# Decayed attention into a softplus FFN: later units load k and q in 32x32 blocks, and their new state is computed as whole-float32 products

## The chip, the cores and the metric

The kernel runs on one core of a Trainium2 chip. The metric is the device time of one execution in microseconds (us). The engines are PE (matrix products), DVE (vector), ACT (scalar), POOL (GpSimd) and SP, which here only issues transfers (DMAs). Each has a queue of its own that it works off in order; semaphores order the engines among each other.

## The reference, cut to what matters

```python
# q, k, v: (4, 8, 768, 64) float32; w_in: 512 x 2048, w_out: 2048 x 512, in float64
gamma = 1.0 - 2.0 ** (-5.0 - arange(H))
for t in range(S):
    state = gamma * state + einsum('bhd,bhe->bhde', k[:, :, t], v[:, :, t])
    y[:, :, t] = scale * einsum('bhd,bhde->bhe', q[:, :, t], state)
x = y.transpose(0, 2, 1, 3).reshape(3072, 512)
h = x @ w_in
out = (maximum(h, 0) + log1p(exp(-abs(h)))) @ w_out
```

Per head, the attention carries a 64x64 state that decays by gamma with each position. Its output, 3072 tokens of 512, goes through a two-layer FFN with softplus between the layers.

## The kernel before

**Units.** The attention is cut into chunks of 128 positions. A unit is one chunk of one batch for one half of the heads (`hf`, four heads, which are `NJ` = 2 pairs): 4 batches x 6 chunks x 2 halves = 48 units. A unit goes through parts, at the distances in ticks that `PARTS` gives (four ticks from unit to unit):

- `load_unit`: k, q and v of the unit come in as `kn`, `qn`, `vn`, positions on the partitions, one DMA each on SP's queue. `kn` and `qn` have two buffers, `vn` three (`vns`).
- `decay`: POOL multiplies `qn` and `vn` by tables of powers of gamma (`qtabs`, `vtabs`).
- `operands`: PE transposes `kn` and `qn` by pairs of heads into one PSUM tile `tp` (four transposes, L152 and L154), so that the head dimension lies on the partitions.
- `scores`: products of k and q, masked by POOL into `ah` (and `al`).
- `new_state`: the product of k and v is added to a running state in PSUM, `stp`. The last chunk of a batch skips it.
- `stack_and_outputs`: the output `yp`, then copies of the state for the next chunk.

**Early and later units.** Units below `WHOLE` = 12 use whole float32 operands. From unit 12 on, each operand is split into a high part rounded to float32r (a cast on ACT) and the rest (a subtraction on DVE): `kq` for k and q, `vhl` for v, `kh` and `kl` for k as it is needed in `new_state`. A product is then a sum of three: high x high, high x low, low x high.

**FFN.** The 3072 tokens are handled in nine blocks (`BLOCKS`), 2048 hidden features in 16 groups. `hidden` is the first layer (L310 to L312: three products of 128x384 or 128x256 each), `softplus_1` and `softplus_2` run on DVE, ACT and POOL, `second` is the other layer (L341 to L343, 128x512). Until about 110 us the weights also come in and are split (`load_weights`, `convert_weights`).

**What sets the order.** The loops interleave attention ticks and FFN steps by `plan`, and a list scheduler with its own timeline then sets the final order on each engine. On PE the units' products stand between those of the FFN. All loads and stores share SP's queue. Every DMA of SP and ACT uses one of eight semaphores (named DMAHW0 to DMAHW7 in the order below) and waits until the one that used it last has landed.

Of the kernel before, what the change touches and what calls it, by code (L numbers as in the profile page):

```python
# [10 lines left out]
F32 = mybir.dt.float32  # L11
F32R = mybir.dt.float32r
# [3 lines left out]
ALU = mybir.AluOpType  # L16

P = 128
C = 128
# [6 lines left out]
WHOLE = 12  # L26
# [7 lines left out]
def decay_attention_then_softplus_ffn(ctx: ExitStack, tc: tile.TileContext, q, k, v, w_in, w_out, qtab, vtab, gtab, out):  # L34
    nc = tc.nc
    B, H, S, D = q.shape
    DM, DF = w_in.shape
    NC = S // C
# [5 lines left out]
    HH = H // 2  # L44
    NJ = HH // 2

    const = ctx.enter_context(tc.tile_pool(name="const", bufs=1))
    attn = ctx.enter_context(tc.tile_pool(name="attn", bufs=1))
# [8 lines left out]
    gtab_sb = const.tile([P, 2, H], F32, name="gtab_sb")  # L57
    qtabs = const.tile([P, NC, H], F32, name="qtabs")
    vtabs = const.tile([P, NC, H], F32, name="vtabs")
    ident = const.tile([P, P], F32, name="ident")  # L60


# [38 lines left out]
    units = [(c // NC, c % NC, hf) for c in range(B * NC) for hf in range(2)]  # L101
    loads, live, state = {}, {}, {}
# [4 lines left out]
    for i, size in enumerate(BLOCKS):  # L107
        at = (0, 256, 384, 0)[i] if i < 4 else 384 * (i % 2 == 0)
# [4 lines left out]
    lo, up = slice(0, D), slice(D, P)  # L113
# [12 lines left out]
    stp = ps_s.tile([P, 2, NJ, P], F32, name="stp")  # L126
    sides = ((0, lo, up), (1, up, lo))

    def load_unit(n):
        if n in loads:  # L130
            return
        b, c, hf = units[n]
        tiles = []
        for nm, src in (("kn", k), ("qn", q), ("vn", v)):
            t = vns[n % 3][:, :, 0, :] if nm == "vn" else attn.tile([P, HH, D], F32, name=nm, bufs=2)
            nc.sync.dma_start(t, src[b, hf * HH:(hf + 1) * HH, c * C:(c + 1) * C, :].rearrange("h s d -> s h d"))
            tiles.append(t)
        loads[n] = tiles

    def decay(n):  # L140
        b, c, hf = units[n]
        kn, qn, vn = loads[n]
        hs = slice(hf * HH, (hf + 1) * HH)
        nc.gpsimd.tensor_tensor(qn, qn, qtabs[:, c, hs].unsqueeze(2).broadcast_to([P, HH, D]), op=ALU.mult)  # L144
        nc.gpsimd.tensor_tensor(vn, vn, vtabs[:, c, hs].unsqueeze(2).broadcast_to([P, HH, D]), op=ALU.mult)  # L145

    def operands(n):
        b, c, hf = units[n]
        kn, qn, vn = loads.pop(n)
        tp = ps_a.tile([P, 2, NJ, C], F32, name="tp", tag="a")  # L150
        for j in range(NJ):
            nc.tensor.transpose(tp[:, 0, j, :], kn[:, 2 * j:2 * j + 2, :], ident)  # L152
        for j in range(NJ):
            nc.tensor.transpose(tp[:, 1, j, :], qn[:, 2 * j:2 * j + 2, :], ident)  # L154
        if n < WHOLE:
            qt = qs[:, n % 2]
            nc.scalar.copy(kz[lo, 0], tp[lo, 0])
            nc.vector.tensor_copy(kz[up, 1], tp[up, 0])
            nc.scalar.copy(qt, tp[:, 1])
            live[n] = [qt, kn, vn]  # L160
            return
        kq = kqs[n % 2]
        for par, own, oth in sides:
            nc.scalar.copy(kq[own, :2, par], tp[own])  # L164
            nc.scalar.copy(kq[oth, 1, par], tp[own, 1])  # L165
        for par, own, oth in sides:
            nc.vector.tensor_tensor(kq[oth, 0, par], tp[own, 0], kq[own, 0, par].bitcast(F32), op=ALU.subtract)  # L167
            nc.vector.tensor_tensor(kq[own, 2, par], tp[own, 1], kq[own, 1, par].bitcast(F32), op=ALU.subtract)

        vhl = attn.tile([P, HH, 2, D], F32R, name="vhl", tag="vhl", bufs=2)  # L170
        nc.scalar.copy(vhl[:, :, 0, :], vn)
        nc.vector.tensor_tensor(vhl[:, :, 1, :], vn, vhl[:, :, 0, :].bitcast(F32), op=ALU.subtract)
        kh = kl = None
        if c < NC - 1:
            kh = attn.tile([P, HH, D], F32R, name="kh", tag="kh")
            kl = attn.tile([P, HH, D], F32R, name="kl")
            nc.scalar.copy(kh, kn)
            nc.vector.tensor_tensor(kl, kn, kh.bitcast(F32), op=ALU.subtract)
        live[n] = [kq, vhl, kh, kl]

    def scores(n):
        kq = live[n][0]
# [23 lines left out]
    began = {}  # L206

    def new_state(n):
        b, c, hf = units[n]
        live[n].append(state[hf] if c else None)  # L210
        if c == NC - 1:
            return
        for j in range(NJ):
            hs = slice(2 * j, 2 * j + 2)
            if n < WHOLE:
                kn, vn = live[n][1:3]
                products = [(kn, vn)]
            else:
                vhl, kh, kl = live[n][1:4]
                vh, vl = (vhl[:, :, t, :] for t in range(2))  # L220
                products = [(kh, vh), (kh, vl), (kl, vh)]
            for i, (kk, vv) in enumerate(products):

                first = c == 0 and hf == 0 and j == 0 and i == 0
                m = nc.tensor.matmul(  # L225
                    stp[:, hf, j, :], lhsT=kk[:, hs, :], rhs=vv[:, hs, :], start=first, stop=True, skip_group_check=True
                )
                if first:
                    began[b] = m.ins
                elif c == 0:  # L230
                    tc.add_manual_dep(m.ins, began[b].name, mybir.DependencyInfo(mybir.DependencyClass.NoSync, mybir.DependencyReason.DATA), reason="the bank's first")

    def stack_state(n):
        b, c, hf = units[n]
# [14 lines left out]
    def outputs(n):  # L249
        b, c, hf = units[n]  # L250
        kq, *rest, st = live.pop(n)
        off, g = places[n // 2], hf * NJ
        xh, xl = (x[:, g:g + NJ, off:off + C] for x in xring)
        if n < WHOLE:
            kn, vn, a = rest
            yp = ps_a.tile([P, NJ, C], F32, name="yp", tag="a")
            v0 = vns[n % 3].rearrange("p h t d -> p (h t) d")
            for j in range(NJ):
                if c:
                    nc.tensor.matmul(yp[:, j], lhsT=st[:, j, :], rhs=kq[:, j, :], start=True, stop=False)  # L260
                for par in range(2):
                    at = 2 * (2 * j + par) - par
                    nc.tensor.matmul(yp[:, j], lhsT=v0[:, at:at + 2, :], rhs=a[:, 2 * j + par, :], start=c == 0 and par == 0, stop=par == 1)
            nc.scalar.copy(xh, yp)  # L264
            nc.vector.tensor_tensor(xl, yp, xh.bitcast(F32), op=ALU.subtract)
            return
        yp = ps_a.tile([D, 2, NJ, C], F32, name="yp", tag="a")
        vhl, kh, kl, ah, al = rest
        for j in range(NJ):
            for par in range(2):  # L270
                h = 2 * j + par
                o = yp[:, par, j, :]
                if c:
                    nc.tensor.matmul(o, lhsT=st[:, par, j, :], rhs=kq[:, 1, par, j, :], start=True, stop=False)  # L274
                    nc.tensor.matmul(o, lhsT=st[:, par, j, :], rhs=kq[:, 2, par, j, :], start=False, stop=False)  # L275
                nc.tensor.matmul(o, lhsT=vhl[:, h, 0, :], rhs=ah[:, h, :], start=c == 0, stop=False)  # L276
                nc.tensor.matmul(o, lhsT=vhl[:, h, 0, :], rhs=al[:, h, :], start=False, stop=False)  # L277
                nc.tensor.matmul(o, lhsT=vhl[:, h, 1, :], rhs=ah[:, h, :], start=False, stop=True)  # L278
        for par, own, oth in sides:
            nc.scalar.copy(xh[own], yp[:, par])  # L280
        for par, own, oth in sides:
            nc.vector.tensor_tensor(xl[own], yp[:, par], xh[own].bitcast(F32), op=ALU.subtract)
# [8 lines left out]
    PERIOD = 4  # L291
# [72 lines left out]
    for i, a, b in turns:  # L364
        m = WIDE // BLOCKS[i]
        steps += [(i, tuple(range(f, f + m))) for f in range(a, b, m)]

    def ticks_for(i):

        return min(PERIOD * 2 * int(FIRST[i + 1] // C) + max(PARTS) - PERIOD + 1 + AHEAD, last_tick + 1)  # L370

    done, loaded, converted = FIRST_TICK, 0, 0
# [11 lines left out]
    for n in range(2):  # L384
        load_unit(n)
# [16 lines left out]
    for c in range(1, NC):  # L402
        nc.vector.tensor_tensor(qtabs[:, c], qtabs[:, c - 1], gtab_sb[:, 0], op=ALU.mult)
        nc.vector.tensor_tensor(vtabs[:, c], vtabs[:, c - 1], gtab_sb[:, 1], op=ALU.mult)
    while done < ticks_for(0):
        tick(done)
        done += 1
        if done % 4 == 3 and done > 0 or done < 0 and loaded == 0:
            if loaded >= FETCH:
                convert_weights(converted)  # L410
                converted += 1
            load_weights(loaded)
            loaded += 1
# [3 lines left out]
    for a, b in zip(starts, starts[1:]):  # L417
        i = steps[b][0]
# [61 lines left out]
```

## Time and profile before

| | us |
|---|---|
| median of 3 runs | 690.71 (690.22 to 691.65) |
| the profiled execution | 691.96 |
| its span, first to last instruction | 690.2 |
| granted TensorE clock, mean | 0.997 |

The profile is of one execution. Busy time counts each engine by itself; the engines overlap. A row of a group gives the line, engine, operation, output and inputs with shapes, the count, then busy time and the mean of one in ns, then idle time just before these instructions and what ended it. Rows of a timeline begin with start and duration in us. SPq and ACTq are the sequencers that issue DMAs.

### The profile page before, as it was taken

Reading aid. Unit: us, or ns where it says so; the run is one execution under the profiler, and the core shown is the slowest. Engines: PE = TensorE matmul, PEld = TensorE weight load, DVE = VectorE, ACT = ScalarE, POOL = GpSimd, SP = SyncE. Lnnn points to the kernel's source line nnn. Section 1 sums busy time; section 2 is a strip of 40 time slices with the busy share of each in tenths; the row PEclk is TensorE's granted clock in tenths of the full one; section 3 lists DMA queues with packets and bytes.
Section 4 is the critical chain, followed back from the end, with each engine's and each line's share of the span. In section 5 each row is a group of like instructions: output and inputs, shape, how many; then the busy total and the mean of one; then the engine's idle time right before and its main releaser. Section 6 shows DMA issues by size and latency. Waiting matters only on the chain.

```text
span 690.2 us, 12071 instructions
## 1 busy us (share of the span) xinstructions
PE 675.2 (98%) x4340; PEld 618.9 (90%) x4340; DVE 417.0 (60%) x873; ACT 354.5 (51%) x802; POOL 283.0 (41%) x344
## 2 busy tenths in 40 slices
PE   6899999999999999999999999999999999999997
PEld 5798999999999999999999999999999999999996
DVE  5687785756656665566666666666766555533321
ACT  5788775555545544545545546455554544433221
POOL 5687675334443334343433433343333423222221
PEclk9999999999999999999999999999999999999999
DMA  8977632121111121112111121111211101000100
GB/s 244 287 221 223 175 127 47 39 69 55 32 23 39 25 77 24 39 24 62 41 37 24 31 69 39 25 31 27 82 32 24 24 15 62 1 0 1 47 1 30
DMA packets 90746, 42.72 MB, mean 62 GB/s; under 512 B 77376, under 2 KB 85568, under 8 KB 90688
## 3 DMA queue, kind: packets, MB, share of 16 engines
q1 hardware_dynamic: 90240, 41.96, 22.2%
q8 instruction: 34, 0.56, 0.3%
q14 instruction: 24, 0.20, 0.1%
q10 hardware_dynamic: 448, 0.01, 0.0%
HBM read 35.66 MB, written 6.29 MB: 61 GB/s over the span
## 4 chain that ended last, share of the span: by engine, by line
PE 94%; DMA 3%; ACT 1%; SPq 1%; POOL 1%; issue 0%; POOLq 0%
PE hp L310 13%; PE acc L341 13%; PE hp L312 13%; PE hp L311 13%; PE acc L343 13%; PE acc L342 13%; PE stp L225 3%; PE sc L195 3%; PE tp L154 1%; PE tp L152 1%; PE yp L278 1%; PE yp L277 1%; PE yp L276 1%; DMA kn<-in_k_dram 1%; PE yp L275 1%; PE yp L274 1%
## 5 line engine op out<-in xcount | busy, mean ns | idle before, releaser
L326 POOL TENSOR_TENSOR gl<-sp,gh 128x384 fp32r<-128x384 f32 (+1 forms) x120 | 129.2, 1077 | 184.7 <-ACT gh L324 147.6
L310 PE MATMUL hp<-xh,winhl 128*128 128x384 f32 (+1 forms) x576 | 185.9, 323 | 0.5 <-ACT xh L264 0.5
L312 PE MATMUL hp<-xh,winhl 128*128 128x384 f32 (+1 forms) x576 | 184.0, 320 | 0.4 <-POOL winhl L98 0.4
L311 PE MATMUL hp<-xl,winhl 128*128 128x384 f32 (+1 forms) x576 | 183.7, 319 | 0.0
L341 PE MATMUL acc<-wouthl,gh 128*128 128x512 f32 x384 | 154.6, 403 | 0.0
L342 PE MATMUL acc<-wouthl,gh 128*128 128x512 f32 x384 | 151.2, 394 | 0.0
L343 PE MATMUL acc<-wouthl,gl 128*128 128x512 f32 x384 | 150.3, 394 | 0.1
L317 DVE TENSOR_SCALAR sp<-hp 128x384 uint32<-128x384 uint32 (+1 forms) x120 | 69.7, 582 | 111.0 <-PE hp L312 105.7
L318 ACT ACTIVATE sp<-sp 128x384 f32<-128x384 f32 (+1 forms) x120 | 65.4, 546 | 124.1 <-DVE sp L317 123.4
L310 PEld LDWEIGHTS hp<-xh,winhl 128*128 128x128 f32 x576 | 108.8, 189 | 3.9 <-ACT xh L264 0.7
L311 PEld LDWEIGHTS hp<-xl,winhl 128*128 128x128 f32 x576 | 108.9, 189 | 3.2
L312 PEld LDWEIGHTS hp<-xh,winhl 128*128 128x128 f32 x576 | 108.8, 189 | 1.2 <-POOL winhl L98 0.6
L324 ACT CAST gh<-sp 128x384 fp32r<-128x384 f32 (+1 forms) x120 | 64.1, 534 | 86.6 <-DVE sp L322 44.3
L322 DVE SCALAR_TENSOR_TENSOR sp<-hp,sp 128x384 f32<-128x384 f32 (+1 forms) x120 | 69.8, 582 | 34.6 <-ACT sp L318 33.5
L343 PEld LDWEIGHTS acc<-wouthl,gl 128*128 128x128 f32 x384 | 71.8, 188 | 15.0 <-POOL gl L326 0.5
L342 PEld LDWEIGHTS acc<-wouthl,gh 128*128 128x128 f32 x384 | 72.5, 189 | 11.0
L341 PEld LDWEIGHTS acc<-wouthl,gh 128*128 128x128 f32 x384 | 72.3, 188 | 10.5
L144 POOL TENSOR_TENSOR qn<-qn,qtabs 128x256 f32<-128x256 f32 x48 | 29.5, 615 | 97.6 <-DMA qn<-in_q_dram 79.0
L167 DVE TENSOR_TENSOR kq<-tp,kq 64x256 fp32r<-64x256 f32 x72 | 30.4, 422 | 61.3 <-ACT kq L165 60.7
L164 ACT CAST kq<-tp 64x512 fp32r<-64x512 f32 x72 | 41.8, 581 | 38.7 <-PE tp L154 37.7
L145 POOL TENSOR_TENSOR vn<-vn,vtabs 128x256 f32<-128x256 f32 x48 | 29.8, 621 | 67.2 <-DMA vn<-in_v_dram 50.4
L201 POOL TENSOR_SCALAR_AFFINE_SELECT ah<-ah 128x512 fp32r<-128x512 f32 (+1 forms) x48 | 31.4, 654 | 33.3 <-DVE al L198 26.3
(81 smaller groups left out, 1044.6 us busy)
## 6 DMA issues: line engine op xcount, KB each, us to landing
win<-in_moe_w_in_dram SPq DMA_DIRECT2D x16, 512.0 KB, 4.4
wout<-in_moe_w_out_dram SPq DMA_DIRECT2D x16, 512.0 KB, 4.5
kn<-in_k_dram SPq DMA_DIRECT2D x48, 128.0 KB, 2.3
qn<-in_q_dram SPq DMA_DIRECT2D x48, 128.0 KB, 2.7
vn<-in_v_dram SPq DMA_DIRECT2D x48, 128.0 KB, 2.2
out_dram<-o SPq DMA_DIRECT2D x24, 256.0 KB, 2.1
gtab_sb<-in_gtab_dram ACTq DMA_DIRECT2D x2, 2.0 KB, 3.2
qtabs<-in_qtab_dram ACTq DMA_DIRECT2D x1, 4.0 KB, 2.2
```

The lines of the kernel that those rows point to most:

```text
L164: nc.scalar.copy(kq[own, :2, par], tp[own])
L310: nc.tensor.matmul(hp[:, k], lhsT=wt[:, 0, d, :], rhs=xh[:, d, :], start=d == 0, stop=False)
L311: nc.tensor.matmul(hp[:, k], lhsT=wt[:, 0, d, :], rhs=xl[:, d, :], start=False, stop=False)
L312: nc.tensor.matmul(hp[:, k], lhsT=wt[:, 1, d, :], rhs=xh[:, d, :], start=False, stop=d == ND - 1)
L317: nc.vector.tensor_scalar(sp.bitcast(U32), hps[s].bitcast(U32), 0x80000000, None, op0=ALU.bitwise_or)
L318: nc.scalar.activation(sp, sp, AF.Softplus)
L322: nc.vector.scalar_tensor_tensor(g, hps.pop(s), 0.0, g, op0=ALU.max, op1=ALU.add)
L324: nc.scalar.copy(gh, g)
L326: nc.gpsimd.tensor_tensor(gl, sps.pop(s), gh.bitcast(F32), op=ALU.subtract)
L341: nc.tensor.matmul(acc[i][t], lhsT=gh[:, k, ts], rhs=wt[:, 0], start=begins and k == 0, stop=False)
L342: nc.tensor.matmul(acc[i][t], lhsT=gh[:, k, ts], rhs=wt[:, 1], start=False, stop=False)
L343: nc.tensor.matmul(acc[i][t], lhsT=gl[:, k, ts], rhs=wt[:, 0], start=False, stop=ends and f == fs[-1])
```

## The change

**Loads.** For later units q comes in 32x32 blocks instead of as `qn`, and k comes a second time, in blocks, beside `kn`: tiles `kb` and `qb` (`qb` takes the two buffers of `qn`). `load_blocks` issues eight DMAs for each, one per head and half of its 64 columns; a DMA moves 32 x 4 x 32 numbers, in runs of 32 (128 bytes). A later unit has 18 load DMAs on SP instead of three.

**Transposes.** DVE transposes `kb` and `qb` block by block, straight into the PSUM tile `tp`, which gets the same contents as before. PE transposes only the early units.

**Decay.** The positions of q now lie differently, so POOL multiplies `qb` by another table, `qblocks`. Its first chunk is loaded by 16 small DMAs on ACT's queue and extended to the other chunks by ten products on POOL (`block_decays`, called in the first loop after 16 ticks are done).

**New state.** Later units compute it like the early ones, with two float32 products per unit, one per pair of heads, out of `kn` and `vn`; `kh` and `kl` are gone. `kn` and `vn` are now held until then.

```diff
+    def load_blocks(nm, src, b, c, hf):
+        t = attn.tile([P, NJ, C // 32, 32], F32, name=nm, tag={"qb": "qn"}.get(nm, nm), bufs=2)
+        for h in range(HH):
+            for d in range(0, D, 32):
+                at = h % 2 * D + d
+                nc.sync.dma_start(
+                    t[at:at + 32, h // 2], src[b, hf * HH + h, c * C:(c + 1) * C, d:d + 32].rearrange("(i t) d -> t i d", t=32)
+                )
+        return t
...
         for nm, src in (("kn", k), ("qn", q), ("vn", v)):
+            if nm == "qn" and n >= WHOLE:
+                for nm, src in (("kb", k), ("qb", q)):
+                    tiles.append(load_blocks(nm, src, *units[n]))
+                continue
...
+            qb = loads[n][2].rearrange("p m i d -> p (m i) d")
+            by = qblocks[:, c, hf].rearrange("p m i -> p (m i)")
+            nc.gpsimd.tensor_tensor(qb, qb, by.unsqueeze(2).broadcast_to(list(qb.shape)), op=ALU.mult)
...
-        for j in range(NJ):
-            nc.tensor.transpose(tp[:, 0, j, :], kn[:, 2 * j:2 * j + 2, :], ident)
-        for j in range(NJ):
-            nc.tensor.transpose(tp[:, 1, j, :], qn[:, 2 * j:2 * j + 2, :], ident)
         if n < WHOLE:
+            for t, x in enumerate((kn, *rest)):
+                for j in range(NJ):
+                    nc.tensor.transpose(tp[:, t, j, :], x[:, 2 * j:2 * j + 2, :], ident)
...
+        for t, x in enumerate(rest):
+            nc.vector.transpose(tp[:, t].rearrange("p j c -> p (j c)"), x.rearrange("p m i d -> p (m i d)"))
...
-        if c < NC - 1:
-            kh = attn.tile([P, HH, D], F32R, name="kh", tag="kh")
-            kl = attn.tile([P, HH, D], F32R, name="kl")
-            nc.scalar.copy(kh, kn)
-            nc.vector.tensor_tensor(kl, kn, kh.bitcast(F32), op=ALU.subtract)
...
-                products = [(kh, vh), (kh, vl), (kl, vh)]
...
+            m = nc.tensor.matmul(
+                stp[:, hf, j, :], lhsT=kn[:, hs, :], rhs=vn[:, hs, :], start=first, stop=True, skip_group_check=True
+            )
...
+    def block_decays():
+        own = (lo, slice(0, H, 2)), (up, slice(1, H, 2))
+        for at in range(0, P, 32):
+            for i in range(C // 32):
+                nc.scalar.dma_start(
+                    qblocks[at:at + 32, 0, :, :, i].rearrange("p f m -> p (f m)"), qtab[i * 32:(i + 1) * 32, at // D:H:2]
+                )
...
+        if done == PERIOD * 4:
+            block_decays()
```

The scheduler sets the order anew. Three places matter. The first is ACT's queue in the start, with the semaphore waits in brackets. Before, behind the four loads of tables, it stands so (`kz`, `qs`: operands of the first units; `stw`: state; `ah`: scores; `win`, `wout`: weights):

```order
L157 COPY kz<-tp 64x256 [waits PE_49]
L159 COPY qs<-tp 128x256 [waits DVE_49]
L241 COPY stw_87<-stp 64x2x64 [waits DVE_49]
L188 COPY ah<-sc 128x512 [waits PE_49]
L85 ACTIVATE win<-win 128x512 [waits DMAHW2_49]
```

In the changed kernel, at the same place:

```order
L420 DMA qblocks<-in_qtab_dram 32x4x1 [waits DMAHW1_49]
L178 COPY kz<-tp 64x256 [waits PE_49]
L420 DMA qblocks<-in_qtab_dram 32x4x1 [waits DMAHW3_49]
L180 COPY qs<-tp 128x256 [waits DVE_49]
L420 DMA qblocks<-in_qtab_dram 32x4x1 [waits DMAHW5_49]
L251 COPY stw_88<-stp 64x2x64 [waits DVE_49]
L420 DMA qblocks<-in_qtab_dram 32x4x1 [waits DMAHW7_49]
L420 DMA qblocks<-in_qtab_dram 32x4x1 [waits DMAHW1_49]
L205 COPY ah<-sc 128x512 [waits PE_49]
L86 ACTIVATE win<-win 128x512 [waits DMAHW4_49]
```

The 16 loads of `qblocks` are spread over the first 44 instructions of ACT, up to the weights of the third group; each waits for an earlier one, and ACT with it. They take the odd semaphores, so that SP's first loads share the even ones.

The second place is SP's queue in the middle of the program. Before, three loads a unit:

```order
L136 DMA kn<-in_k_dram 128x4x64
L136 DMA qn<-in_q_dram 128x4x64
L136 DMA vn_90<-in_v_dram 128x4x64
L136 DMA kn<-in_k_dram 128x4x64
L136 DMA qn<-in_q_dram 128x4x64
```

In the changed kernel:

```order
L152 DMA kn<-in_k_dram 128x4x64
L136 DMA kb<-in_k_dram 32x4x32 x4
L136 DMA qb<-in_q_dram 32x4x32 x8
L152 DMA vn_92<-in_v_dram 128x4x64
L152 DMA kn<-in_k_dram 128x4x64
L136 DMA kb<-in_k_dram 32x4x32 x8
L136 DMA qb<-in_q_dram 32x4x32 x8
```

Sixteen block loads stand between one `kn` and the next. The first blocks, `kb` of units 12 and 13, have moved far ahead, between the loads of units 5 to 7.

The third place is DVE's queue in the middle. Before (`sp`: softplus of one FFN step; `kq`: the split k and q of a unit; `kl`: the low part of k; `st`: state):

```order
L317 TENSOR_SCALAR sp<-hp 128x384
L167 TENSOR_TENSOR kq_83<-tp,kq_83 64x256
L168 TENSOR_TENSOR kq_83<-tp,kq_83 64x256
L167 TENSOR_TENSOR kq_83<-tp,kq_83 64x256
L168 TENSOR_TENSOR kq_83<-tp,kq_83 64x256
L322 SCALAR_TENSOR_TENSOR sp<-hp,sp 128x384
L178 TENSOR_TENSOR kl<-kn,kh 128x256
```

In the changed kernel:

```order
L327 TENSOR_SCALAR sp<-hp 128x384
L184 STREAM_TRANSPOSE tp<-kb 128x256
L184 STREAM_TRANSPOSE tp<-qb 128x256
L332 SCALAR_TENSOR_TENSOR sp<-hp,sp 128x384
L190 TENSOR_TENSOR kq_85<-tp,kq_85 64x256
L191 TENSOR_TENSOR kq_85<-tp,kq_85 64x256
```

The two transposes stand between the two softplus operations of an FFN step, ahead of the corrections of `kq` that need them, and the subtraction for `kl` is gone.

More of the change, by code (lines that the diff above doesn't have):

```diff
@@ L59, in decay_attention_then_softplus_ffn @@
     vtabs = const.tile([P, NC, H], F32, name="vtabs")
+    qblocks = const.tile([P, NC, 2, NJ, C // 32], F32, name="qblocks")
     ident = const.tile([P, P], F32, name="ident")
@@ L141, in decay @@
         b, c, hf = units[n]
-        kn, qn, vn = loads[n]
+        vn = loads[n][-1]
         hs = slice(hf * HH, (hf + 1) * HH)
-        nc.gpsimd.tensor_tensor(qn, qn, qtabs[:, c, hs].unsqueeze(2).broadcast_to([P, HH, D]), op=ALU.mult)
+        if n < WHOLE:
+            qn = loads[n][1]
+            nc.gpsimd.tensor_tensor(qn, qn, qtabs[:, c, hs].unsqueeze(2).broadcast_to([P, HH, D]), op=ALU.mult)
+        else:
+            qb = loads[n][2].rearrange("p m i d -> p (m i) d")
+            by = qblocks[:, c, hf].rearrange("p m i -> p (m i)")
+            nc.gpsimd.tensor_tensor(qb, qb, by.unsqueeze(2).broadcast_to(list(qb.shape)), op=ALU.mult)
         nc.gpsimd.tensor_tensor(vn, vn, vtabs[:, c, hs].unsqueeze(2).broadcast_to([P, HH, D]), op=ALU.mult)
@@ L148, in operands @@
         b, c, hf = units[n]
-        kn, qn, vn = loads.pop(n)
+        kn, *rest, vn = loads.pop(n)
         tp = ps_a.tile([P, 2, NJ, C], F32, name="tp", tag="a")
-        for j in range(NJ):
-            nc.tensor.transpose(tp[:, 0, j, :], kn[:, 2 * j:2 * j + 2, :], ident)
-        for j in range(NJ):
-            nc.tensor.transpose(tp[:, 1, j, :], qn[:, 2 * j:2 * j + 2, :], ident)
         if n < WHOLE:
+            for t, x in enumerate((kn, *rest)):
+                for j in range(NJ):
+                    nc.tensor.transpose(tp[:, t, j, :], x[:, 2 * j:2 * j + 2, :], ident)
             qt = qs[:, n % 2]
@@ L172, in operands @@
         nc.vector.tensor_tensor(vhl[:, :, 1, :], vn, vhl[:, :, 0, :].bitcast(F32), op=ALU.subtract)
-        kh = kl = None
-        if c < NC - 1:
-            kh = attn.tile([P, HH, D], F32R, name="kh", tag="kh")
-            kl = attn.tile([P, HH, D], F32R, name="kl")
-            nc.scalar.copy(kh, kn)
-            nc.vector.tensor_tensor(kl, kn, kh.bitcast(F32), op=ALU.subtract)
-        live[n] = [kq, vhl, kh, kl]
+        live[n] = [kq, vhl, kn, vn]
     def scores(n):
@@ L212, in new_state @@
             return
+        kn, vn = live[n][1:3] if n < WHOLE else live[n][2:4]
         for j in range(NJ):
             hs = slice(2 * j, 2 * j + 2)
[L215 to L220, printed above, removed]
-                products = [(kh, vh), (kh, vl), (kl, vh)]
[L222 to L231, printed above, removed]
+            first = c == 0 and hf == 0 and j == 0
+            m = nc.tensor.matmul(
+                stp[:, hf, j, :], lhsT=kn[:, hs, :], rhs=vn[:, hs, :], start=first, stop=True, skip_group_check=True
+            )
+            if first:
+                began[b] = m.ins
+            elif c == 0:
+                tc.add_manual_dep(m.ins, began[b].name, mybir.DependencyInfo(mybir.DependencyClass.NoSync, mybir.DependencyReason.DATA), reason="the bank's first")
     def stack_state(n):
@@ L267, in outputs @@
         yp = ps_a.tile([D, 2, NJ, C], F32, name="yp", tag="a")
-        vhl, kh, kl, ah, al = rest
+        vhl, kn, vn, ah, al = rest
         for j in range(NJ):
@@ L404, in decay_attention_then_softplus_ffn @@
         nc.vector.tensor_tensor(vtabs[:, c], vtabs[:, c - 1], gtab_sb[:, 1], op=ALU.mult)
+    def block_decays():
[5 more added lines that the diff above has]
+                )
+        for c in range(1, NC):
+            for half, heads in own:
+                old, new = (qblocks[half, t].rearrange("p f m i -> p (f m) i") for t in (c - 1, c))
+                nc.gpsimd.tensor_tensor(new, old, gtab_sb[half, 0, heads].unsqueeze(2).broadcast_to(list(new.shape)), op=ALU.mult)
     while done < ticks_for(0):
```

## The prediction

> **What bounds the kernel now.** I read the page first (span, busy times, chain that ended last), then busy time by stretches, and only then the order of work on TensorE.
>
> ```profile
> span 690.2 us, 12071 instructions
> ...
> PE 675.2 (98%) x4340; PEld 618.9 (90%) x4340; DVE 417.0 (60%) x873; ACT 354.5 (51%) x802; POOL 283.0 (41%) x344
> ...
> PE 94%; DMA 3%; ACT 1%; SPq 1%; POOL 1%; issue 0%; POOLq 0%
> ```
>
> The matmul engine (PE) is busy for 675.2 of 690.2 us and makes 94% of the chain. A busy PE alone could hide slack, so the second view says where it is ever idle. Its columns are the stretch, its length, then busy time of PE, weight loads, DVE, ACT and POOL, the granted clock, the DMA share and GB/s.
>
> ```profile
> 0.00:10.00 10.00, 5.26 (x21) 4.31 (x22) 3.77 (x19) 2.98 (x6) 4.91 (x17) 1.00 0.78 205
> 10.00:20.00 10.00, 6.40 (x45) 5.44 (x44) 6.87 (x13) 8.26 (x19) 5.96 (x8) 1.00 1.03 296
> 20.00:30.00 10.00, 8.14 (x54) 7.78 (x55) 7.10 (x13) 6.81 (x16) 6.87 (x9) 0.83 1.04 303
> ...
> 200.00:400.00 200.00, 200.00 (x1274) 183.84 (x1273) 125.96 (x277) 101.99 (x245) 76.40 (x98) 1.00 0.15 37
> ...
> 640.00:690.20 50.20, 46.34 (x291) 41.70 (x290) 13.07 (x19) 11.16 (x18) 10.33 (x8) 1.00 0.07 27
> ```
>
> Of the 15.0 us without PE work, 10.2 lie in the first 30 us (4.74 + 3.60 + 1.86) and 3.9 in the last stretch. In between PE runs without a hole (200.00 of 200.00), while DVE has 37% free, ACT 49% and the DMA engines 85%. So there are two regimes: after the start, each nanosecond of PE issue time that goes is a nanosecond of the span; in the start, what counts is ACT and the loads.
>
> **What goes from PE.** In the pipelined order an instruction costs the distance to the next start, not its own duration. The timeline of PE (start, duration) around the four transposes of one later unit:
>
> ```profile
> 302.52 0.35 PE L310 MATMUL hp<-xh,winhl 128*128 128x384 f32 x1
> 302.70 0.34 PE L311 MATMUL hp<-xl,winhl 128*128 128x384 f32 x1
> 302.88 0.34 PE L312 MATMUL hp<-xh,winhl 128*128 128x384 f32 x1
> 303.06 0.38 PE L152 MATMUL tp<-ident,kn 128*128 128x128 f32 x2
> 303.28 0.38 PE L154 MATMUL tp<-ident,qn 128*128 128x128 f32 x2
> 303.42 0.42 PE L310 MATMUL hp<-xh,winhl 128*128 128x384 f32 x1
> 303.67 0.34 PE L311 MATMUL hp<-xl,winhl 128*128 128x384 f32 x1
> ```
>
> Two 128x384 products are 0.18 us apart. From 302.88 to 303.67 stand two of them and the four transposes: 0.79 - 2 x 0.18 = 0.43 us. There are 36 later units (12 to 47), so **36 x 0.43 = 15.5 us** go.
>
> The new state of a later unit, six products of two pairs of heads:
>
> ```profile
> 325.27 0.33 PE L311 MATMUL hp<-xl,winhl 128*128 128x384 f32 x1
> 325.45 0.33 PE L225 MATMUL stp<-vhl,kh 128*128 128x128 f32 x2
> 325.62 0.27 PE L225 MATMUL stp<-vhl,kl 128*128 128x128 f32 x1
> 325.73 0.39 PE L225 MATMUL stp<-vhl,kh 128*128 128x128 f32 x2
> 325.95 0.27 PE L225 MATMUL stp<-vhl,kl 128*128 128x128 f32 x1
> 326.06 0.45 PE L341 MATMUL acc<-wouthl,gh 128*128 128x512 f32 x1
> 326.35 0.40 PE L342 MATMUL acc<-wouthl,gh 128*128 128x512 f32 x1
> 326.58 0.40 PE L195 MATMUL sc<-kq 128*128 128x256 f32 x2
> ```
>
> From 325.27 to 326.35 is 1.08 us; less 0.18 for L311 and 0.23 for a 128x512 product (326.35 to 326.58) it leaves 0.67 us for the six. What takes their place, whole-float32 products, the early units already run:
>
> ```profile
> 42.19 0.61 PE L225 MATMUL stp<-vn,kn 128*128 128x128 f32 x4
> 42.64 0.38 PE L152 MATMUL tp<-ident,kn 128*128 128x128 f32 x2
> ...
> L225 PE MATMUL stp<-vn,kn 128*128 128x128 f32 x40 | 7.2, 307 | 0.0
> ```
>
> 40 instructions for 10 early units: each of a unit's two products is two instructions, and the four take 0.45 us (42.19 to 42.64). The exchange saves 0.67 - 0.45 = 0.22 us. It happens in 30 units, since the last chunk of a batch makes no state (six of the 36): **30 x 0.22 = 6.6 us**. Together 22.1 us.
>
> The Trainium skill speaks against this half: "FP8 and Floating Point Precision", section "TensorE Precision Notes", has true float32 take four passes through the array, against the three products that it replaces here. Four passes at the 0.11 us of one split product would be 2 x 4 x 0.11 = 0.89 us a unit, 0.22 more than now, and the sum of PE would be 15.5 - 6.6 = 8.9 us. The rows differ: four instructions in 0.45 us. That the passes are four they don't contradict; a split product of 128 columns simply costs as much as two of them.
>
> **What is added beside PE.** DVE gets two 32x32-block transposes of 128x256 per unit; the trace has none. ACT loses the copy kh and DVE the subtraction kl in 30 units.
>
> ```profile
> L168 DVE TENSOR_TENSOR kq<-tp,kq 64x256 fp32r<-64x256 f32 x72 | 30.4, 422 | 1.0
> L178 DVE TENSOR_TENSOR kl<-kn,kh 128x256 fp32r<-128x256 f32 x30 | 19.2, 640 | 6.3 <-ACT kh L177 6.3
> ...
> 330.20 0.38 PE L152 MATMUL tp<-ident,kn 128*128 128x128 f32 x2
> ```
>
> Nearest rows for 256 elements a partition: 0.42 (out of PSUM) to 0.64 us; I take 0.43, so DVE gets 36 x 0.86 - 30 x 0.64 = 12 us more in all. A unit lasts (330.20 - 303.06) / 2 = 13.6 us here; at 63% DVE has 5.0 us of it free. The pair stands in DVE's queue between the first and second softplus operation of one FFN step, so these and the corrections of kq wait behind it: about 0.9 us later, hidden by other products that PE has queued. I cost it at nothing; without that cover it is 36 x 0.86 = 31 us. POOL's decay keeps its size, 128x256.
>
> The loads: sixteen transfers of 16 KB take the place of one of 128 KB.
>
> ```profile
> 303.47 0.37 SPq L136 DMA_DIRECT2D kn<-in_k_dram  x1
> 303.94 0.45 SPq L136 DMA_DIRECT2D qn<-in_q_dram  x1
> ...
> L136 SPq DMA_DIRECT2D qn<-in_q_dram x48: 367/448/1312, 1.3 to 569.0; - x48
> ...
> DMA to landing us min/median/max: 2.3/2.7/7.4
> ...
> q1 hardware_dynamic: 90240, 41.96, 22.2%
> ```
>
> SP needs 0.37 to 0.45 us for one, so 18 loads a unit take 6.7 to 8.1 of 13.6 us: SP keeps up. kn now waits for the new-state products of two units before (it waited for kl), and kb and qb queue behind it; but a unit's qn is issued just after the transposes two units earlier (303.94 behind 303.28), some 27 us ahead, and vn, now held until the new state, has three buffers. Sixteen issues, a landing of 2.7 and a decay use about 11 of these. In packets it is 36 x 1536 = 55,296 more, at the present cost of a packet 22.2% x 55,296 / 90,240 = 14% more share of engines that are idle there. Cost nothing; what uncovers it is below.
>
> **What is added in the start.** Sixteen transfers for the block decays stand in ACT's own queue, and 16 blocks of kb for units 12 and 13 among the first loads of SP.
>
> ```profile
> 0.84 0.43 ACTq L387 DMA_DIRECT2D qtabs<-in_qtab_dram  x1
> ...
> 2.43 0.60 ACTq L390 DMA_DIRECT2D gtab_sb<-in_gtab_dram  x1
> ...
> PE sc L187 <- ACT qs L159: 2.3, 5, 0.8
> ```
>
> At the mean of these two, 0.52 us, ACT spends 8.3 us on issuing, interleaved with the copies for which PE waits: the last row has PE waiting five times for qs. Bounds: 0 if all of it falls in ACT's idle time, 8.3 us if none does. Five issues stand ahead of the first ah, where ACT is mostly idle (it is busy for 2.98 us of the first 10); the other eleven, 5.7 us, share a stretch in which ACT is 68 to 83% busy. I take **4.5 us**, with the start's loads inside it: SP's transfers now alternate semaphores with ACT's, so each waits for an earlier one, and the weights of the first FFN steps come some microseconds later. Gains below nothing I exclude: nothing leaves the start.
>
> **Sum.** -15.5 - 6.6 + 4.5 = -17.6 us: a span of 672.6 for the 690.2. The profiled execution took 691.96 us with its ends, 1.25 above the median of 690.71. Against the median: 690.7 - 17.6 = **673.1 us**.
>
> **Rivals.** (1) The start costs nothing: 690.7 - 22.1 = 668.6. For it: the gaps of ACT there; against it: PE's waits for qs.
> (2) DVE's transposes come late for the scores. If each unit's scores waited 0.2 us for kq, 7.2 us come back: 680; if as long as the PE transposes took, 0.43 us, 15.5 come back: 688.6, nearly no change, and the change then does not do what it says. Against it: 5.0 us of DVE free per unit.
> (3) A float32 product costs four split ones (0.89 us a unit): 690.7 - 15.5 + 6.6 + 4.5 = 686.3. Against it: the rows of the early units, 0.45 us.
> (4) The slower side: block loads don't keep pace. The transfers share eight semaphores (DMAHW0 to 7 in the order), so eight are under way at most, and 18 a unit need 18/8 of a landing: 6.1 us at 2.7. PE will need 13.6 - 0.43 - 0.22 = 13.0 us a unit, so the loads bind from a landing of 13.0 x 8/18 = 5.8 us, and have eaten the whole gain, the 4.5 us of the start counted (0.1 a unit), at 13.5 x 8/18 = 6.0. Landings up to 7.4 us stand in the row above, and the start has the DMA share at 1.03; in the middle it is 0.15. At 7 us a unit takes 15.75: 690.7 + 4.5 + 36 x 2.15 = 773 us.
>
> The Trainium skill, "DMA: Bandwidth & Descriptors", section "Anatomy of one DMA — SWDGE (gpsimd) path", puts a fixed cost of about 2.0 us on each transfer whatever its size, which speaks for (4) if they follow each other singly: an estimate of 16 x 2.0 = 32 us a unit. By that rule the trace agrees in size, 2.3 us at least; it does not agree that they queue, since qn was issued 0.47 us behind kn.
>
> **How the numbers follow.** Forecast, PE full and the start dearer by 2 to 8.3 us: 0.62 (670 to 677). (1): 0.14. (2): 0.13, of which 0.03 ends within 0.2% of no change. (3): 0.02. (4): 0.06. Something else in the new order that costs over 5 us but stays faster: 0.03. The range from 667.5, a little below (1) for a differently packed order, to 681.5, with the milder half of (2), leaves out under 0.2. Faster by over 0.2% (what a measurement of this kernel can tell from no change): 0.91; within: 0.03; slower: 0.06. The likeliest time, 673.1, is that of the first case.
>
> **What would show it.** Right: no transposes on PE from unit 12 on, four new-state instructions of 0.11 us where six stood, PE still 200.00 busy of any 200 us in the middle, and idle time in the first 30 us up from 10.2 to about 15. Wrong: PE rows with idle time ended by ACT kq or DVE (2), SP or DVE waiting for DMA kb or qb (4), first FFN products still near 25 us (1). The step that I trust least is the 4.5 us.

## The result and the profile after

| | before | changed |
|---|---|---|
| median us | 690.71 (689.88 to 691.65, 5 runs) | 696.33 (693.88 to 697.0, 5 runs) |
| profiled execution, us | 691.96 | 694.59 |
| its span, us | 690.2 | 692.8 |
| ratio of the times | | 1.007, 95% interval 1.0047 to 1.0093 |

The change made the kernel 0.7% slower. Forecast were 673.1 us and a range of 667.5 to 681.5. First the page of the changed kernel: span, busy times, shares of the chain.

```profile
span 692.8 us, 12604 instructions
...
PE 661.2 (95%) x4136; PEld 600.2 (87%) x4136; DVE 419.2 (61%) x915; ACT 343.1 (50%) x772; POOL 285.1 (41%) x354
...
PE 82%; DMA 6%; DVE 5%; ACT 3%; issue 2%; POOL 1%; SPq 1%; ACTq 0%; DVEq 0%; POOLq 0%
```

PE has 204 records fewer, as it should (4340 - 4136), and 14.0 us less busy time; yet its share of the chain fell from 94% to 82%, and DVE, DMA and ACT came in. The span grew by 2.6 us. The same stretches as before the change:

```profile
0.00:10.00 10.00, 5.34 (x23) 4.28 (x24) 3.54 (x19) 2.94 (x6) 4.92 (x17) 1.00 0.75 187
10.00:20.00 10.00, 3.95 (x29) 3.33 (x29) 6.12 (x12) 6.23 (x14) 4.51 (x9) 0.98 0.89 213
20.00:30.00 10.00, 8.85 (x58) 7.97 (x56) 5.91 (x11) 7.25 (x17) 7.43 (x12) 0.85 0.90 249
200.00:400.00 200.00, 196.90 (x1216) 178.73 (x1215) 128.64 (x296) 98.09 (x236) 77.17 (x99) 1.00 0.24 47
640.00:692.80 52.80, 49.21 (x307) 44.20 (x305) 13.07 (x19) 11.67 (x19) 11.35 (x9) 0.99 0.07 26
```

Two things differ. PE is idle for 11.9 us of the first 30 (10.2 before), and the middle has holes: 196.90 of 200 us, where it had been 200.00. Idle time understates a stall, since the first products behind it are stretched too. So the second measure is the time between two events that every version has: the copies of finished blocks by DVE, `o`. The rows give count, duration, and the first and last start. Before:

```profile
L355 DVE COPY o<-acc x14: 680/692/693, 137.8 to 685.7; 128x512 f32<-128x512 f32 x14
```

In the changed kernel:

```profile
L365 DVE COPY o<-acc x14: 681/688/692, 143.0 to 688.6; 128x512 f32<-128x512 f32 x14
```

The first copy is 5.2 us late. From the first to the last it takes 545.6 us in place of 547.9: 2.3 us were saved there, out of some 21 (worked out below). Where the others went is seen in PE's waits (total, times, longest):

```profile
PE yp L284 <- DVE al L216: 2.9, 4, 0.9
PE yp L284 <- DVE kq L191: 2.6, 1, 2.6
...
PE yp L287 <- POOL al L218: 1.4, 5, 0.3
PE sc L212 <- DVE kq L191: 1.2, 2, 0.9
```

Before, PE had no wait at all from 100 to 640 us. The waits lie near 160, 242, 325, 407, 490 and 574 us: once a block of 384 tokens, where one block's FFN ends and the next begins. I call these places seams. The largest, on DVE (start, duration):

```profile
400.95 0.42 DVE L216 TENSOR_TENSOR al<-sc,al 128x256 fp32r<-128x256 f32 x1
...
401.89 0.45 DVE L184 STREAM_TRANSPOSE tp<-kb 128x256 f32<-128x256 f32 x1
402.37 0.46 DVE L184 STREAM_TRANSPOSE tp<-qb 128x256 f32<-128x256 f32 x1
404.16 0.69 DVE L365 COPY o<-acc 128x512 f32<-128x512 f32 x1 [1.32 <-DMA out_dram<-o]
...
406.64 0.43 DVE L191 TENSOR_TENSOR kq<-tp,kq 64x256 fp32r<-64x256 f32 x1
407.10 0.42 DVE L215 TENSOR_TENSOR al<-sc,ah 128x256 fp32r<-128x256 f32 x1
```

And on PE at the same time:

```profile
402.43 0.48 PE L212 MATMUL sc<-kq 128*128 128x256 f32 x2
...
404.32 0.34 PE L322 MATMUL hp<-xh,winhl 128*128 128x384 f32 x1
407.22 0.24 PE L284 MATMUL yp<-kq,st 128*64 128x128 f32 x1 [2.56 <-DVE kq L191]
407.30 0.22 PE L285 MATMUL yp<-kq,st 128*64 128x128 f32 x1
408.35 0.27 PE L286 MATMUL yp<-ah,vhl 128*64 128x128 f32 x1 [0.83 <-POOL ah L218]
408.60 0.49 PE L320 MATMUL hp<-xh,winhl 128*128 128x384 f32 x1
408.89 0.52 PE L321 MATMUL hp<-xl,winhl 128*128 128x384 f32 x1
409.21 0.52 PE L322 MATMUL hp<-xh,winhl 128*128 128x384 f32 x1
```

A unit's scores come in two pairs of heads, each with its own buffer of a PSUM pool that has two; `tp` and `yp` take theirs from the same pool. At 400.95 the last row of `al` for the unit's first pair starts. Then come the transposes for the next unit, 401.89, and only then this unit's second scores, 402.43. The outputs `yp`, next in PE's queue but for products of the FFN, wait until 407.07 for the last correction of `kq` of the next unit (L191): that is the last reader of `tp`, so `yp` takes over its buffer. Before the change, PE's own queue had the order scores, scores, `tp`, `yp`; the transposes were behind both scores because the same engine ran both.

At four of the other five seams (units 20, 26, 38 and 44) the outputs' first wait is for `al` itself. Near 242 us, on DVE and on PE:

```profile
238.97 0.46 DVE L184 STREAM_TRANSPOSE tp<-kb 128x256 f32<-128x256 f32 x1
239.47 0.46 DVE L184 STREAM_TRANSPOSE tp<-qb 128x256 f32<-128x256 f32 x1
...
241.40 0.41 DVE L216 TENSOR_TENSOR al<-sc,al 128x256 fp32r<-128x256 f32 x1
```

```profile
238.91 0.48 PE L212 MATMUL sc<-kq 128*128 128x256 f32 x2
239.23 0.34 PE L321 MATMUL hp<-xl,winhl 128*128 128x384 f32 x1
...
240.80 0.34 PE L322 MATMUL hp<-xh,winhl 128*128 128x384 f32 x1
241.96 0.24 PE L284 MATMUL yp<-kq,st 128*64 128x128 f32 x1 [0.82 <-DVE al L216]
```

Here the transposes start behind the second scores (238.97 against 238.91), as they do at the seams of units 26, 38 and 44, so `tp` takes no buffer between the scores there. `yp` waits for the second pair's last `al`, which comes late in DVE's queue. Between the scores and the outputs PE's queue holds ten products, some 1.9 us. Counted through the whole order at the distances of the rows, the first unit of each block has little more than that: 3.3 us for unit 14, and 1.9 each for 20, 26, 32, 38 and 44. All other later units have about 5.2 or more; before the change none had less than 5.0. At unit 14, near 160 us, no output waits; the next scores wait 0.3 us for `al`. (The distances named in the expectations below were counted with eight chunks to a batch, where there are six; the counts here are the right ones, and smaller at some units.)

One execution among the experiments, the profiled one of AHEAD = 0, took 1676 us where its other three took 703.56 to 704.61; its trace is not used below.

### The profile page after: what moved, and what is told of

Its sections match the earlier page's. It is cut to its first block, busy times and chain, and to the rows that moved or that the text cites. A ratio compares the mean times of both kernels' runs of the same rounds, so it can differ in the third digit from the quotient of the medians.

```text
span 692.8 us, 12604 instructions
## 1 busy us (share of the span) xinstructions
PE 661.2 (95%) x4136; PEld 600.2 (87%) x4136; DVE 419.2 (61%) x915; ACT 343.1 (50%) x772; POOL 285.1 (41%) x354
## 4 chain that ended last, share of the span: by engine, by line
PE 82%; DMA 6%; DVE 5%; ACT 3%; issue 2%; POOL 1%; SPq 1%; ACTq 0%; DVEq 0%; POOLq 0%
PE hp L320 12%; PE hp L322 12%; PE acc L351 12%; PE acc L352 12%; PE acc L353 12%; PE hp L321 12%; PE sc L212 2%; DMA qblocks<-in_qtab_dram 2%; PE stp L235 2%; DMA wout<-in_moe_w_out_dram 2%; DMA win<-in_moe_w_in_dram 1%; PE yp L287 1%; PE yp L288 1%; PE yp L286 1%; PE yp L273 1%
## 5 line engine op out<-in xcount | busy, mean ns | idle before, releaser
L218 POOL TENSOR_SCALAR_AFFINE_SELECT ah<-ah 128x512 fp32r<-128x512 f32 (+1 forms) x48 | 30.6, 637 | 117.1 <-DVE al L215 104.8
L166 POOL TENSOR_TENSOR qb<-qb,qblocks 128x256 f32<-128x256 f32 x36 | 22.2, 618 | 54.4 <-DMA qb<-in_q_dram 45.5
L292 DVE TENSOR_TENSOR xl<-yp,xh 64x256 fp32r<-64x256 f32 x72 | 30.0, 417 | 17.4 <-ACT xh L290 16.5
```

## The experiments

Times are medians; each ratio is to the kernel before, run on the same chip in turn. The last two columns are the busy time of PE in the first 100 us and from 100 to 640 us of the profiled execution (88.81 and 540.00 before, 82.97 and 529.05 in the changed kernel).

Theories: (1) DVE's queue is too full at the seams; (2) the block loads delay the stores, and so the seams; (3) the new state does it; and, formed on the way, (4) the order in which the transposes now stand; (5) the third output copy, which waits in DVE's queue for a store.

| run | us | ratio (95% interval) | 0 to 100 | 100 to 640 |
|---|---|---|---|---|
| new state alone | 683.77 | 0.9894 (0.9874 to 0.9913) | 89.49 | 540.00 |
| one load each | 687.95 | 0.9949 (0.9929 to 0.9968) | 87.37 | 531.39 |
| 4 loads of decays | 691.92 | 1.0008 (0.9994 to 1.0022) | 87.60 | 528.72 |
| copies on ACT | 695.2 | 1.0057 (1.0033 to 1.008) | 84.59 | 528.67 |
| AHEAD = 0 | 704.24 | 1.0181 (1.0154 to 1.0209) | | |
| AHEAD = 0, 4 loads of decays | 700.03 | 1.0128 (1.0096 to 1.016) | 86.86 | 522.08 |
| spare transposes | 684.52 | 0.9905 (0.9876 to 0.9934) | 89.01 | 540.00 |
| new state alone, AHEAD = 0 | 686.08 | 0.9923 (0.9899 to 0.9948) | 88.34 | 539.28 |
| transposes behind `al` | 678.34 | 0.9808 (0.978 to 0.9836) | 83.75 | 540.00 |
| the same, 4 loads of decays | 673.26 | 0.9736 (0.9706 to 0.9766) | 87.07 | 540.00 |
| third copy's own buffer | 690.98 | 1.0002 (0.9972 to 1.0032) | 84.72 | 532.03 |
| transposes behind the scores | 679.87 | 0.9853 (0.9805 to 0.9901) | 83.41 | 537.62 |

**New state alone.** The kernel before, with this part of the change only:

```diff
-            for i, (kk, vv) in enumerate(products):
...
+            m = nc.tensor.matmul(
+                stp[:, hf, j, :], lhsT=kn[:, hs, :], rhs=vn[:, hs, :], start=first, stop=True, skip_group_check=True
+            )
```

> The kernel before with the whole-float32 new state alone: k and q are loaded in one piece each and transposed by TensorE as before, no block loads, no block decays, no VectorE transposes. Theory 1 (the 19 us that were lost after 100 us are VectorE's two transposes standing in its queue at the block seams; the 6 us in the start are the block decays): nothing of this is here, so the whole saving of the products stays: 690.7 - 6.6 = 684.1 us (683 to 685.5), no TensorE wait over 0.5 us at the seams near 160, 240, 320, 400. Theory 2 (block loads delay the output stores and so the seams): the same, 684. Theory 3 (the seams are lost to the new state's products, which hold kn and vn longer and come in another order): stalls at the seams here too, 690 us or more.

683.77 us, and PE full from 100 to 640. This part kept all it saved and makes no seam. Theory 3 falls.

**One load each for k and q.**

```diff
-        for h in range(HH):
-            for d in range(0, D, 32):
...
+        nc.sync.dma_start(
+            t.rearrange("p m i d -> p (m i d)").rearrange("p (h d) -> p h d", d=D), src[b, hf * HH:(hf + 1) * HH, c * C:(c + 1) * C, :].rearrange("h s d -> s h d")
+        )
```

> The changed kernel with one transfer for each of k and q in place of sixteen; the bytes land in the layout of whole heads, not of blocks, so the arrangement in blocks (and with it the right scores) is left out, while every instruction of the five engines but SyncE's issues is the same. SyncE issues 2 x 15 transfers a unit fewer. Theory 1 (VectorE's queue): the seams keep their stalls, 692 to 696 us, at most 1 to 2 us back in the start. Theory 2 (the 32 block loads a unit hold up the output stores and the loads behind them): the seams close, 676 to 680 us.

The edit takes 14 transfers a unit away, eight to one for each of k and q (the expectation's 30 and 32 are wrong), and it leaves out the blocks, so the outputs are not those of the reference. 687.95 us, which neither theory had. Against the changed kernel PE has 4.4 us more in the first 100 and only 2.3 more in the middle, where 8.6 us of holes stay at the same seams. So the many loads cost something, mostly in the start, and don't make the seams.

**Four loads of the block decays.**

```diff
-            for i in range(C // 32):
-                nc.scalar.dma_start(
-                    qblocks[at:at + 32, 0, :, :, i].rearrange("p f m -> p (f m)"), qtab[i * 32:(i + 1) * 32, at // D:H:2]
-                )
+            nc.scalar.dma_start(
+                qblocks[at:at + 32, 0].rearrange("p f m i -> p (f m) i"), qtab[:, at // D:H:2].rearrange("(i t) m -> t m i", t=32)
+            )
```

> The changed kernel with the block decays fetched by 4 transfers on ScalarE's queue in place of 16; nothing else. The start of the changed kernel lost 6.0 us against the one before. If ScalarE's issues (0.5 us each) are its cost, 12 x 0.5 = 6 us of issuing go and 3 to 5 us of time come back: 691 to 693 us, TensorE busier in the first 60 us. If the start is lost to something else (SyncE's 16 KB loads ahead of the weights), the time stays at 694 to 697. Seams: as in the changed kernel by every theory.

691.92 us, 4.4 less than the changed kernel, and as expected in the start. The first 100 us of the changed kernel and of this run:

```profile
0.00:100.00 100.00, 82.97 (x578) 75.90 (x579) 68.55 (x131) 69.09 (x142) 67.84 (x92) 0.98 0.81 219
```

```profile
0.00:100.00 100.00, 87.60 (x603) 79.79 (x604) 72.79 (x138) 72.51 (x146) 70.82 (x94) 0.98 0.83 223
```

**All output copies on ACT.**

```diff
-                (nc.scalar.copy if t % 2 else nc.vector.tensor_copy)(o, acc[i][t])
+                nc.scalar.copy(o, acc[i][t])
```

> The changed kernel with all four output copies of a block on ScalarE, where two of the four stood on VectorE (0.69 us each). Theory 1 (VectorE's queue at the seams): 1.4 us less stand there ahead of the row al and the corrections of kq, so the stalls at the seams shrink by half or more: 683 to 690 us. Theory 2 (loads and stores) and theory 3 (new state): no change, 693 to 697 us. If ScalarE then becomes late with ah or the copies of kq, the waits name ScalarE in place of VectorE and the time stays.

695.2 us: no gain. This was the first blow to theory 1, though not a clean one, since the scheduler also moved other work.

**AHEAD = 0, alone and with the four loads.**

> The changed kernel with AHEAD = 0 in place of 2 (attention runs two ticks less ahead of the FFN), the same instructions in another order. Theory 1 as first put (VectorE's queue at the seams is simply too full) has lost ground, since taking two output copies off VectorE gave nothing. Theory 4, new: it is the order. In TensorE's queue of the changed kernel the outputs of the first unit of each block (14, 20, 26, 32, 38, 44) stand only 1.9 to 4.5 us of products behind that unit's last scores, where the kernel before has 5.9 to 14; the way from scores over ah, al and the masks to the outputs is longer than that. With AHEAD = 0 these distances are 3.1 (unit 20) to 8.2. Theory 4: the 18 us of the seams shrink to 5 or less, 680 to 685 us. Theory 1: 692 to 697.

> The run before with the block decays fetched by 4 transfers in place of 16. If the two costs (seams, start) are apart, the 4.4 us of the run with 4 transfers come off again: 676 to 680 us by theory 4, which would beat the kernel with the new state alone (683.8); by theory 1 690 to 693.

Both missed: 704.24 and 700.03 us, slower than the changed kernel. The second's waits show why.

```profile
PE hp L320 <- DVE sp L332: 13.3, 7, 2.0
PE hp L320 <- DMA out_dram<-o: 3.6, 3, 1.2
```

PE now waits at the same seams, but for the softplus of the new block's first steps. At 409 to 411 us DVE runs the two transposes between the softplus operations that free the buffers of `hp`. The distance had only grown from 1.9 to 3.1 us; so the miss doesn't refute theory 4, but it shows that the order can also be made worse while the transposes may stand anywhere.

**Spare transposes.** The kernel with the new state alone, with VectorE's transposes added for nobody:

```diff
+        for x in (kn, qn):
+            spare = attn.tile([P, HH * D], F32, name="spare")
+            nc.vector.transpose(spare, x.rearrange("p h d -> p (h d)"))
```

> The kernel with the new state alone (683.8 us; TensorE transposes k and q) plus two 128x256 block transposes by VectorE in every later unit into a spare buffer that nothing reads: VectorE's 0.92 us a unit with nobody waiting for the result, and TensorE's order nearly that of the run without them. Theory 1 (VectorE's time is what the seams lose): stalls at the seams here too, 690 to 700 us. Theory 4 (the order of TensorE's queue): 683 to 686.

The transposes as measured (min, median, max in ns, first and last start), and the middle:

```profile
L164 DVE STREAM_TRANSPOSE spare<-kn x36: 434/446/449, 79.6 to 578.0; 128x256 f32<-128x256 f32 x36
L164 DVE STREAM_TRANSPOSE spare<-qn x36: 423/440/447, 83.8 to 578.5; 128x256 f32<-128x256 f32 x36
```

```profile
100.00:640.00 540.00, 540.00 (x3432) 495.33 (x3431) 342.01 (x758) 260.21 (x610) 199.07 (x252) 1.00 0.14 36
```

72 transposes, 32 us of DVE, cost 0.75 us (684.52 against 683.77, within the spread of both), and PE has no hole. DVE's busy time of 342.01 is above the 337.54 that it has in the changed kernel. PE's order here keeps 4.9 us or more between scores and outputs at the first units of the blocks. So DVE's time alone isn't what the seams lose: theory 1, as it was put, falls.

**New state alone with AHEAD = 0**, the control:

> The kernel with the new state alone and AHEAD = 0: the control to the first run of these four. Its first units keep 4.0 us or more between scores and outputs either way. Theory 4: no gain from AHEAD here, 683 to 687 us. If AHEAD = 0 saves several us here too, what it gains in the changed kernel isn't the seams.

686.08 us: no gain, as theory 4 had it. By the right count its unit 14 has a distance of under 2 us, and this run has the one hole of the kernels with TensorE's transposes: 0.7 us in the middle (539.28 of 540), where `yp` waits for `al`. So a short distance makes a hole even where PE does the transposes.

**Transposes behind the last `al` of the unit before.** One edge of order, `last[n]` being the second L216 of unit n:

```diff
-            nc.vector.transpose(tp[:, t].rearrange("p j c -> p (j c)"), x.rearrange("p m i d -> p (m i d)"))
+            m = nc.vector.transpose(tp[:, t].rearrange("p j c -> p (j c)"), x.rearrange("p m i d -> p (m i d)"))
+            if n - 1 in last:
+                tc.add_manual_dep(m.ins, last[n - 1].name, mybir.DependencyInfo(mybir.DependencyClass.NoSync, mybir.DependencyReason.DATA), reason="behind al")
```

> The changed kernel with one edge of order: a unit's two VectorE transposes stand behind the last row al of the unit before, the same instructions otherwise. In the changed kernel they stand, in every unit from 13 on, between the two rows al of the unit before: so tp takes one of the two buffers of its PSUM pool between the two pairs of scores (4 to 8 us apart in TensorE's queue, 1 to 5 before), and the next unit's copies and corrections of kq go ahead of ah and al. With the edge every unit has 4.4 us or more of products between its last scores and its outputs (1.9 to 2.8 at the seams without). Theory 4 in this form: the seams' 18 us shrink to under 4, 676 to 682 us. Theory 1 (too much work on VectorE at the seams): 690 to 697. If delaying the transposes makes the scores late in every unit: PE waits for kq from the middle of the blocks on, over 700.

678.34 us. Its middle and its copies (L217 and L218 are the two rows of `al` here):

```profile
100.00:640.00 540.00, 540.00 (x3374) 494.32 (x3373) 349.69 (x775) 267.36 (x621) 207.43 (x258) 1.00 0.22 47
```

```profile
L367 DVE COPY o<-acc x14: 667/692/694, 143.6 to 672.0; 128x512 f32<-128x512 f32 x14
```

The same instructions as in the changed kernel, 18.0 us faster (696.33 - 678.34). All holes are gone; first to last copy takes 528.4 us in place of 545.6. The first units of the blocks have 3.5 us (unit 14), then 4.8 to 10.0. At one seam, on DVE:

```profile
247.95 0.41 DVE L217 TENSOR_TENSOR al<-sc,ah 128x256 fp32r<-128x256 f32 x1
248.40 0.42 DVE L218 TENSOR_TENSOR al<-sc,al 128x256 fp32r<-128x256 f32 x1
248.74 0.45 DVE L184 STREAM_TRANSPOSE tp<-kb 128x256 f32<-128x256 f32 x1
249.22 0.46 DVE L184 STREAM_TRANSPOSE tp<-qb 128x256 f32<-128x256 f32 x1
```

**The same with four loads of the block decays.**

> The run before with the block decays fetched by 4 transfers in place of 16. If the 4.4 us of the start come off on top: 672 to 678 us by theory 4, which would be 1 to 2% faster than the kernel with the new state alone; by theory 1 686 to 693.

673.26 us, the best of all: 2.6% faster than the kernel before (ratio 0.9736, interval 0.9706 to 0.9766).

**A buffer of its own for the third output copy.**

```diff
-            o = ffn.tile([P, DM], F32, name="o", tag="o")
+            o = ffn.tile([P, DM], F32, name="o", tag="part" if t == 2 else "o")
```

> The changed kernel with the third output copy of a block going to another buffer, so that it doesn't wait in VectorE's queue for the first store to land (1.32 us of waiting at 404 us in the changed kernel's profile). The transposes stay between the two rows al. Theory 5 (the blocked queue at the seams is this wait): 683 to 688 us. Theory 4: the short distances at the seams stay, so 691 to 696.

690.98 us, in ten runs from 689.01 to 696.66, and 8.0 us of holes in the middle. It takes at most a third off; the seams aren't this wait.

**Transposes behind the last scores.** The weaker edge, with `last[n]` the last L212 of unit n:

```diff
-                tc.add_manual_dep(m.ins, last[n - 1].name, mybir.DependencyInfo(mybir.DependencyClass.NoSync, mybir.DependencyReason.DATA), reason="behind al")
+                tc.add_manual_dep(m.ins, last[n - 1].name, mybir.DependencyInfo(mybir.DependencyClass.Sync, mybir.DependencyReason.SCHED_ONLY), reason="behind the scores")
```

> The changed kernel with a weaker edge: a unit's transposes wait for the last scores of the unit before, no longer for its last al. On VectorE they still stand between the two rows al of the unit before; but tp takes its PSUM buffer only when both pairs of scores have theirs. TensorE's queue then has 4.4 us or more between a unit's last scores and its outputs. If what counts at the seams is the PSUM buffer that tp takes between the scores (and so the order of TensorE's queue): 676 to 682 us, as with the stronger edge. If it is the place in VectorE's queue, ahead of al: stalls at the seams stay, 686 to 694.

679.87 us, with 2.4 us of holes left; units 14, 26 and 38 keep a distance of only 3.5 to 3.7 us, and the holes are at their seams. There PE's next scores wait, and no output does:

```profile
PE sc L214 <- ACT st L257: 1.3, 2, 0.6
...
PE sc L214 <- DVE kq L193: 0.7, 1, 0.7
```

With the stronger edge unit 14 has 3.5 us too, and no hole. On DVE near 249 us the transposes still stand ahead of the unit's last `al`:

```profile
248.62 0.45 DVE L184 STREAM_TRANSPOSE tp<-kb 128x256 f32<-128x256 f32 x1
248.98 0.40 DVE L217 TENSOR_TENSOR al<-sc,ah 128x256 fp32r<-128x256 f32 x1
249.30 0.43 DVE L184 STREAM_TRANSPOSE tp<-qb 128x256 f32<-128x256 f32 x1
249.64 0.40 DVE L218 TENSOR_TENSOR al<-sc,al 128x256 fp32r<-128x256 f32 x1
```

So their place ahead of `al` in DVE's queue is not what costs most. Two ways are left: the PSUM buffer that `tp` takes between the scores, and the other order of PE's queue that the scheduler makes, with its short distances. The edge changes both, so no run separates them. In the trace of the changed kernel the wait for L191 at 407 us shows the buffer at one seam; at units 20, 26, 38 and 44 the transposes start behind the scores, and what stands there is the short distance together with a late `al`.

## Why the prediction was wrong

**The sum of PE was right.** Between the first and the last output copy two of the 36 later units are already transposed, so 34 x 0.43 + 28 x 0.22 = 20.8 us should go there. With the edge 19.5 went (547.9 - 528.4). The new state by itself took 8.1 us off the median (691.84 - 683.77, against 6.6 forecast). The four passes of the Trainium skill, "FP8 and Floating Point Precision", section "TensorE Precision Notes", priced at 0.11 us each (rival 3), would have made this run slower. It was faster, and the rows of the early units were the better guide to the price.

**The start was a little too cheap.** PE is idle for 17.0 us of the first 100, before for 11.2: 5.8 us, where 4.5 was taken and 8.3 was the bound. The cause was right: four loads in place of sixteen bring back 4.4 us, or 5.1 beside the edge (678.34 - 673.26). That the loads of k and q cost nothing beside it was wrong in the start: one load for each brings PE 4.4 us there. The two aren't additive (together they would be more than was lost), and weren't tried together.

**The failed step is the cost of the moved transposes**: "about 0.9 us later, hidden by other products that PE has queued. I cost it at nothing". As a sum of DVE's time this held: the trace shows 0.457 and 0.451 us for one, 0.43 was taken, and the spare transposes cost nothing that could be measured.

```profile
L184 DVE STREAM_TRANSPOSE tp<-kb 128x256 f32<-128x256 f32 x36 | 16.4, 457 | 0.8
L184 DVE STREAM_TRANSPOSE tp<-qb 128x256 f32<-128x256 f32 x36 | 16.3, 451 | 0.9
```

What failed is that I asked how long DVE would work and not what the transposes had been ordered behind. On PE they stood behind both scores of the unit before, by the queue alone. On DVE nothing held them: in all 35 units that follow a later unit they stand between its two rows of `al`, and in 28 of these they start before its second scores, taking a buffer there. In the middle of a block PE has about 5.2 us and more of products to cover that; in the new order it has 1.9 at five seams and 3.3 at the sixth. I had read the slack (5.0 us of DVE a unit) and the order in the middle of a block, and neither at a seam. The cost was 18.0 us, by the run that undoes it with one edge; with the start's 5.8 it is more than the 22.1 saved. That sum gives 1.7 us slower, where the medians say 5.6 and the profiled spans 2.6; what makes up the rest stays open.

**The rivals.** Nearest was (2), transposes late for the scores, at 680 to 688.6; but its price was per unit and its wait mostly in the wrong place: from 100 to 640 us the outputs wait 7.7 us, at five of the six seams, and the scores 2.1. Rival (4), loads that don't keep pace, did not come: a 16 KB block lands in 1.7 us (median), far from the 5.8 at which they would have bound, and below the 2.0 that the prediction's estimate took as fixed.

```profile
kb<-in_k_dram SPq DMA_DIRECT2D x288, 16.0 KB, 1.7
```

## What to carry to other kernels

When work moves to another engine, ask first what its old queue had silently kept it behind, and whether it can now take a shared buffer earlier; that order has to be written down as an edge. A mean of free time over a period says nothing of the place in the period where two stages meet: read the slack there. And where a scheduler makes the order, one edge can be worth more than the instructions saved: here 18 us against 22.

## What the runs showed of the hardware

One stall cost more than its length. Around the seam at 407 us:

```profile
404.00:408.00 4.00, 0.96 (x6) 0.53 (x4) 3.74 (x9) 1.68 (x4) 0.34 (x1) 1.00 0.74 181
408.00:412.00 4.00, 3.65 (x12) 3.56 (x13) 1.25 (x3) 1.49 (x3) 2.87 (x4) 0.60 0.22 36
```

Behind 2.56 and 0.83 us without products, with two short ones between them, the granted clock is 0.60 over the next 4 us, and 128x384 products stand 0.32 us apart (408.89 to 409.21) that stood 0.18 apart ahead of it (404.14 to 404.32 by the timeline). At the other seams of this run the clock stayed, behind waits of up to 0.95 us.

The Trainium skill, "TensorE: Matmul & The Clock Gate", section "Part 1: The HAM clock gate (the "warmup" mystery)", has the clock halve after an idle window of some 3.4 us. The two waits here are of that size together, 3.39 us, with two products between them. But other runs show the clock fall behind much less. With four loads of the decays it is 0.57 from 321 to 325 us, behind waits of 0.18, 0.31 and 0.92 us within the 4 us ahead; with the third copy's own buffer it is 0.53 from 245.0 to 248.6, behind 0.51, 0.31 and 0.73. So no length of idle time from which on the clock falls can be read from these runs.

How often it falls differs between executions of one kernel. Of the five of the changed kernel, two have a mean clock of 0.995 and spans of 692.1 and 692.8 us, the profiled one among them; the other three have 0.988 to 0.990 and 694.6 to 695.2 us. This may be part of what the sum above leaves open; no run here tests it.
